# A layer whose first token block is run in two halves of eight feature chunks, with partial sums kept in DRAM

## The chip, the core and the metric

The kernel runs on one core of a Trainium2 chip. The metric is the device time of one execution in microseconds (us). The core has a matrix engine (TensorE, PE in the rows; its weight loads are PEld), two elementwise engines (VectorE is DVE, ScalarE is ACT), GpSimd (POOL), and SyncE (SP), which here only issues DMAs. Each engine works through its own instructions in order. [...]

## What is computed

```python
# attention, per batch b and head h, state is D x D
state = gamma[h] * state + k[t]^T v[t];   y[t] = q[t] @ state / sqrt(D)
x  = y as (B*S = 3072 tokens, H*D = 512)
# layer 1
h  = x @ w_in;   g = h * sigmoid(1.702 * h);          x = g @ w_out
# layer 2 (own weights, a and b are small vectors)
h  = x @ w_in2;  g = P(h) / (Q(h) + 1e-6);            out = g @ w_out2
```

Both layers go from 512 to 2048 features and back. The weights arrive as float64 and are used as float32.

## The kernel before

**Tiling.** The 3072 tokens are cut into 24 chunks of 128 for the attention and into 6 blocks of 512 (four chunks) for the layers. The 2048 features are cut into 16 feature chunks of 128 (`KF` = 16). A *step* is one layer, one block and one feature chunk: 2 x 6 x 16 = 192 steps, numbered j = 0 to 191, layer 1 first. In this text hp*j* and z*j* are the tiles of step j.

**A step.** `g1(j)` multiplies the block's input (a high part `xh` and a low part `xl`) with the chunk's input weights into a PSUM tile `hp`: 12 matmuls of 512 columns. In layer 1, `act1_a` and `act1_b` then make the activation: ACT takes the sigmoid (L367), DVE multiplies it to `z` (L368), ACT rounds `z` to `gh` (L373), and DVE makes the rest `gl` (L374). `g2(i)` multiplies `gh` and `gl` with the output weights, 12 more matmuls, and adds them into four PSUM accumulators `o0` to `o3`. Those have one buffer each. `g1` is issued two steps ahead of `g2` (`lead`). After the last feature chunk of a block, `evac` copies the four accumulators to `os` tiles (two buffers) and stores them to `x2d` in DRAM, from where layer 2 reads them (`load_x2`).

**Weights of layer 1.** 32 units, two for each feature chunk (`wi` and `wo`). Each is loaded as float64 words, turned to float32 by one ACT instruction (L125) and four DVE instructions (L131, L132, L133, L135), and split into two parts by one ACT instruction (L146) and one DVE instruction (L147). `prep(upto)` issues these at two units a step, so that they last for the whole first block.

**Attention of a later block** stands beside the steps of the block ahead of it: `todo` gives each block's four chunks twelve units, kinds T (transposes of q and k), S (scores `pS`, masked by DVE to `sm`, L221) and Y (output `pY`, new state `pK`; DVE makes `xl`, L247, and the state `st`, L252 or L254). Y also loads the chunk two places on and scales its q and k (L186), on POOL for chunks 4 to 7 and on DVE from chunk 8 on. Before, they are spread over the first 13 steps of the block ahead.

**Weights of layer 2** are turned to float32 beside later steps of layer 1, one unit every two steps from step `conv0` = 18 on, and stored to DRAM; during the last block of layer 1 they are loaded again and split.

**Order.** The code gives the order in which the work is traced. SP's DMAs keep that order. The other engines' instructions are put in order by a scheduler when the program is built.

Of the kernel before, what the change touches and what calls it, by code (L numbers as in the profile page):

```python
# [9 lines left out]
F32 = mybir.dt.float32  # L10
# [4 lines left out]
ALU = mybir.AluOpType  # L15
PSUM = bass.MemoryType.PSUM
DRAM = bass.MemoryType.DRAM

P = 128
B, H, S, D = 4, 8, 768, 64  # L20
NT, DM, DFF = B * S, H * D, 2048
# [3 lines left out]
KF = DFF // P  # L25
# [2 lines left out]


def constants():  # L30
    """Identity, causal mask and decay tables: they depend on the shapes alone."""
    gamma = 1.0 - 2.0 ** (-5.0 - np.arange(H, dtype=np.float64))
    t = np.arange(S, dtype=np.float64).reshape(NCH, P)
    up = gamma[None, None, :] ** (t[:, :, None] + 1.0) / np.sqrt(D)
    down = gamma[None, None, :] ** -(t[:, :, None] + 1.0)
    i = np.arange(P)
    c = np.concatenate(
        [
            np.eye(P),
            (i[None, :] >= i[:, None]).astype(np.float64),  # L40
            up.transpose(1, 0, 2).reshape(P, NCH * H),
            down.transpose(1, 0, 2).reshape(P, NCH * H),
        ],
        axis=1,
    )
    return np.ascontiguousarray(c.astype(np.float32))
# [3 lines left out]
def tile_kernel(ctx: ExitStack, tc: tile.TileContext, q, k, v, w1i, w1o, w2i, w2o, pa, pb, cst, out):  # L50
    nc = tc.nc
# [8 lines left out]
    io = ctx.enter_context(tc.tile_pool(name="io", bufs=2))  # L60
# [13 lines left out]
    warm = ws.tile([P, 512], mybir.dt.bfloat16, tag="s", name="warm")  # L74
    st = const.tile([P, NP, P], F32, name="st")

# [1 line left out]
    # A unit is half of what a step needs: 512 columns of the input or of the output weights.  # L78
    dr_w = {}
    for nm, shape in (("i", [DM, DFF]), ("o", [DFF, DM])):  # L80
        dr_w[nm] = dr.tile(shape, F32, name="w2" + nm)
# [10 lines left out]
        return ("i", "o")[u % 2], u // 2  # L92

    def stage_tag(u):
        """The first layer's words wait where the weights of later steps will lie."""
        if u < 16:
            at_slot = 31 - u
        elif u < 24:
            at_slot = 47 - u
        elif u < 28:  # L100
            at_slot = 55 - u
        else:
            return None
        return f"w{at_slot}"
# [56 lines left out]
        nc.sync.dma_start(out=m.rearrange("p (c f) -> p c f", c=KD) if nm == "i" else m, in_=view(nm, dr_w[nm], fc))  # L161
        STG[u] = m

# [1 line left out]
    RAW = {}  # L165
    QK = {}
    SM = {}
# [85 lines left out]
                else:  # L253
                    nc.vector.tensor_copy(out=st[r, :, r], in_=pk[r, :, 0:D])  # L254

# [1 line left out]
    blocks = {1: [4] * 6, 2: [4] * 6}  # L257
    steps = []
    starts = {}
    for layer in (1, 2):  # L260
        t0 = 0
        for bi, n in enumerate(blocks[layer]):
            starts[layer, bi] = t0
            for fc in range(KF):
                steps.append((layer, bi, fc, t0, n * P))
            t0 += n * P
    NS = len(steps)
    first = {(s[0], s[1]): i for i, s in reversed(list(enumerate(steps)))}
    lead = {1: 2, 2: 3}

    x2d = dr.tile([DM, NT], F32, name="x2d")
    HP = {}
    G = {}
    CH = {}
# [24 lines left out]
    def g2(j):  # L299
        layer, bi, fc, t0, n = steps[j]  # L300
        gh, gl = G.pop(j)
        wh, wl = W[layer, "o", fc]
        if fc == 0:
            if layer == 1:
                ACC[layer, bi] = [ps_o.tile([P, n], F32, tag=f"o{d}", name=f"o{j}_{d}") for d in range(KD)]
            else:
                ACC[layer, bi] = [ps_o.tile([P, DM], F32, tag=f"o{d}", name=f"o{j}_{d}") for d in range(n // P)]
        acc = ACC[layer, bi]
        a, z = fc == 0, fc == KF - 1
        for d, o in enumerate(acc):  # L310
            r = slice(d * P, (d + 1) * P)
            if layer == 1:
                nc.tensor.matmul(o, wl[:, r], gh, start=a, stop=False)  # L313
                nc.tensor.matmul(o, wh[:, r], gl, start=False, stop=False)  # L314
                nc.tensor.matmul(o, wh[:, r], gh, start=False, stop=z)  # L315
            else:
                nc.tensor.matmul(o, gl[:, r], wh, start=a, stop=False)  # L317
                nc.tensor.matmul(o, gh[:, r], wl, start=False, stop=False)  # L318
                nc.tensor.matmul(o, gh[:, r], wh, start=False, stop=z)  # L319

    def evac(layer, bi, t0, n):
        acc = ACC.pop((layer, bi))
        if layer == 1:
            for d, o in enumerate(acc):
                t = io.tile([P, 512], F32, tag="o", name=f"os{layer}_{bi}_{d}")
                if d % 2:
                    nc.scalar.copy(out=t[:, :n], in_=o)
                else:
                    nc.vector.tensor_copy(out=t[:, :n], in_=o)  # L329
                nc.sync.dma_start(out=x2d[d * P : (d + 1) * P, t0 : t0 + n], in_=t[:, :n])  # L330
            return
        last = bi == len(blocks[2]) - 1
        for d in range(0, n // P, 2):
            t = ws.tile([P, 2, DM], F32, tag="s", name=f"os{layer}_{bi}_{d}")
            for x in range(2):
                if last and x:
                    nc.vector.tensor_copy(out=t[:, x, :], in_=acc[d + x])
                else:
                    nc.scalar.copy(out=t[:, x, :], in_=acc[d + x])
                if last:  # L340
                    nc.sync.dma_start(out=out[t0 + (d + x) * P : t0 + (d + x + 1) * P, :], in_=t[:, x, :])
            if not last:
                rows = out[t0 + d * P : t0 + (d + 2) * P, :].rearrange("(x p) m -> p x m", p=P)
                nc.sync.dma_start(out=rows, in_=t)
# [61 lines left out]
        gh, gl = G[j]  # L406
        nc.vector.scalar_tensor_tensor(out=gl, in0=p, scalar=-1.0, in1=gh.bitcast(F32), op0=ALU.mult, op1=ALU.subtract)

# [1 line left out]
    todo = [[[], []] for _ in range(NS)]  # L410

    def slot_fn(kind, c, tg, bi, o):
# [14 lines left out]
    chunk = blocks[1][0]  # L427
    for bi in range(1, len(blocks[1])):
        n = blocks[1][bi]
        i0 = first[1, bi - 1]  # L430
        room = KF - lead[1] - 1
        units = [(kind, chunk + x, x * P) for x in range(n) for kind in "TSY"]
        for u, (kind, c, o) in enumerate(units):
            pos = u * 2 * room // len(units)
# [2 lines left out]

    NU = 2 * KF
    prepped = [0]
    # A unit's words are loaded when the unit that lay in their place is done.  # L440
    after_split = {}
    tenant = {}
    early = []
    for u in range(NU):
        t = stage_tag(u)
# [7 lines left out]
            tenant[t] = u  # L453

    def prep(upto):
        """Units of the first layer's weights: three stages, each one unit behind the one before."""
        while prepped[0] < min(upto, NU + 2):
            s = prepped[0]
            if s < NU:
# [9 lines left out]
    with tc.manual_schedule(engines={mybir.EngineType.SP}):  # L469
# [69 lines left out]
        nc.scalar.activation(out=ab[:, 6:7], in_=ab[:, 5:6], func=ACTF.Abs)  # L539
        nxt = 0  # L540
        lastb = first[1, len(blocks[1]) - 1]
        conv0 = KF + 2
        for i in range(-lead[1], NS):
            p0 = 2 * (i + lead[1]) + 5
            prep(p0)
            while nxt < NS and nxt - lead[steps[nxt][0]] <= i:
                j = nxt
# [20 lines left out]
                f()  # L568
            g2(i)
            layer, bi, fc, t0, n = steps[i]  # L570
            if fc == KF - 1:
                evac(layer, bi, t0, n)
            for f in todo[i][1]:
                f()
            # layer 2 weights: to f32 in DRAM
            if i >= conv0 - 4 and i % 2 == 0:
                u = (i - conv0) // 2
                if 0 <= u < NU:
# [2 lines left out]
                    w_store(u)  # L581
                if u + 2 < NU:
                    w_load(2, u + 2)
            # layer 2 weights take the places that the last block of layer 1 leaves
            if lastb <= i:
                f = i - lastb
                for u in (2 * f - 2, 2 * f - 1):
                    if 0 <= u < NU:
                        w_split(2, u)
                    if u + 2 < NU:  # L590
                        w_reload(u + 2)
            # inputs of layer 2
            if lastb <= i:
                nb, off = divmod(i - lastb, KF)
                if nb < len(blocks[2]) and off in (3, 6, 9, 12):
# [28 lines left out]
```

## Time and profile before

| what | value |
|---|---|
| median of 3 runs | 1185.49 us (1184.31 to 1185.55) |
| profiled execution, first to last instruction (its span) | 1183.0 us |
| PE busy | 1168.6 us, 99% of the span |
| DVE busy | 845.7 us, 71% |
| ACT busy | 610.4 us, 52% |
| POOL busy | 15.6 us, 1% |

The runs' times stand 1.3 to 2.6 us above the span of the profiled execution, for which only the span is given. In the profile, "busy" of PE counts a matmul until its modelled end, and matmuls overlap; PEld, the weight loads, do not overlap each other. Idle time of an engine is put down to what released it. A DVE instruction of 0.68 us is followed by the next one 0.60 us later when nothing is waited for, since the two overlap.

### The profile page before, as it was taken

Reading aid. Unit: us, or ns where it says so; the run is one execution under the profiler, and the core shown is the slowest. Engines: PE = TensorE matmul, PEld = TensorE weight load, DVE = VectorE, ACT = ScalarE, POOL = GpSimd, SP = SyncE. Lnnn points to the kernel's source line nnn. Section 1 sums busy time; section 2 is a strip of 40 time slices with the busy share of each in tenths; the row PEclk is TensorE's granted clock in tenths of the full one; section 3 lists DMA queues with packets and bytes.
Section 4 is the critical chain, followed back from the end, with each engine's and each line's share of the span. In section 5 each row is a group of like instructions: output and inputs, shape, how many; then the busy total and the mean of one; then the engine's idle time right before and its main releaser. Section 6 shows DMA issues by size and latency. Waiting matters only on the chain.

```text
span 1183.0 us, 15510 instructions
## 1 busy us (share of the span) xinstructions
PE 1168.6 (99%) x6067; PEld 962.7 (81%) x6067; DVE 845.7 (71%) x1372; ACT 610.4 (52%) x1030; POOL 15.6 (1%) x17
## 2 busy tenths in 40 slices
PE   8899999999999999999999999999999999999998
PEld 5787888888888888888888888888888888888887
DVE  6999945545464554553455898888988988988886
ACT  3555523232233323332344876866766766866765
POOL 1100000000000000000000000000000000000000
PEclk9999999999999999999999999999999999999999
DMA  9944233343342423440343200200200200200000
GB/s 255 308 123 114 63 110 88 89 128 86 81 125 77 126 83 101 122 134 1 115 122 109 73 18 1 72 1 1 72 1 1 71 1 1 71 1 1 36 1 36
DMA packets 128600, 89.26 MB, mean 75 GB/s; under 512 B 78224, under 2 KB 111120, under 8 KB 128528
## 3 DMA queue, kind: packets, MB, share of 16 engines
q1 hardware_dynamic: 128528, 88.28, 25.9%
q8 instruction: 47, 0.77, 0.3%
q14 instruction: 25, 0.20, 0.1%
HBM read 67.29 MB, written 20.97 MB: 75 GB/s over the span
## 4 chain that ended last, share of the span: by engine, by line
PE 90%; DVE 8%; issue 1%; DMA 0%; ACT 0%; SPq 0%; POOL 0%
PE hp L294 14%; PE hp L296 14%; PE hp L295 14%; PE o L317 7%; PE o L319 7%; PE o L318 7%; PE o L313 7%; PE o L315 6%; PE o L314 6%; PE pS L217 2%; PE pY L234 2%; DVE u L133 2%; DVE s L135 1%; PE pY L231 1%; DVE s L131 1%; DVE u L132 1%
## 5 line engine op out<-in xcount | busy, mean ns | idle before, releaser
L294 PE MATMUL hp<-xh,wi 128*128 128x512 f32 x768 | 303.4, 395 | 4.9 <-DVE xl L247 2.7
L296 PE MATMUL hp<-xh,wi 128*128 128x512 f32 x768 | 299.7, 390 | 0.0
L295 PE MATMUL hp<-xl,wi 128*128 128x512 f32 x768 | 299.7, 390 | 0.0
L294 PEld LDWEIGHTS hp<-xh,wi 128*128 128x128 f32 x768 | 144.6, 188 | 38.1 <-DVE wi L147 4.5
L296 PEld LDWEIGHTS hp<-xh,wi 128*128 128x128 f32 x768 | 144.6, 188 | 30.7
L295 PEld LDWEIGHTS hp<-xl,wi 128*128 128x128 f32 x768 | 144.6, 188 | 29.0
L367 ACT ACTIVATE z<-hp 128x512 f32<-128x512 f32 x96 | 57.3, 597 | 211.1 <-PE hp L296 210.8
L368 DVE TENSOR_TENSOR z<-hp,z 128x512 f32<-128x512 f32 x96 | 66.1, 688 | 121.8 <-ACT z L367 121.6
L313 PE MATMUL o<-gh,wo 128*128 128x512 f32 x384 | 152.4, 397 | 0.0
L315 PE MATMUL o<-gh,wo 128*128 128x512 f32 x384 | 150.0, 391 | 0.0
L314 PE MATMUL o<-gl,wo 128*128 128x512 f32 x384 | 149.9, 390 | 0.0
L317 PE MATMUL o<-wo,gl 128*128 128x512 f32 x384 | 149.5, 389 | 0.0
L318 PE MATMUL o<-wo,gh 128*128 128x512 f32 x384 | 149.4, 389 | 0.0
L319 PE MATMUL o<-wo,gh 128*128 128x512 f32 x384 | 149.4, 389 | 0.0
L383 ACT ACTIVATE z<-hp 128x512 f32<-128x512 f32 x96 | 57.4, 598 | 145.2 <-PE hp L296 145.2
L386 DVE SCALAR_TENSOR_TENSOR z<-z,ab,w 128x512 f32<-128x512 f32 x96 | 72.0, 750 | 64.0 <-ACT w L384 63.8
L373 ACT CAST gh<-z 128x512 fp32r<-128x512 f32 x96 | 59.8, 623 | 58.8 <-DVE z L368 58.7
L374 DVE TENSOR_TENSOR gl<-z,gh 128x512 fp32r<-128x512 f32 x96 | 66.1, 688 | 29.3 <-ACT gh L373 28.0
L313 PEld LDWEIGHTS o<-gh,wo 128*128 128x128 f32 x384 | 72.1, 188 | 15.9 <-issue 0.2
L315 PEld LDWEIGHTS o<-gh,wo 128*128 128x128 f32 x384 | 72.1, 188 | 15.3
L317 PEld LDWEIGHTS o<-wo,gl 128*128 128x128 f32 x384 | 72.0, 188 | 15.3 <-DVE os L329 0.4
L318 PEld LDWEIGHTS o<-wo,gh 128*128 128x128 f32 x384 | 72.1, 188 | 15.0
(69 smaller groups left out, 1601.7 us busy)
## 6 DMA issues: line engine op xcount, KB each, us to landing
s<-in_moe_w_in_dram SPq DMA_DIRECT2D x32, 512.0 KB, 6.1
s<-in_moe_w_out_dram SPq DMA_DIRECT2D x32, 512.0 KB, 5.9
rawq<-in_q_dram SPq DMA_DIRECT2D x24, 256.0 KB, 4.7
rawk<-in_k_dram SPq DMA_DIRECT2D x24, 256.0 KB, 3.4
rawv<-in_v_dram SPq DMA_DIRECT2D x24, 256.0 KB, 4.0
x2d<-os SPq DMA_DIRECT2D x24, 256.0 KB, 2.1
x<-x2d SPq DMA_DIRECT2D x24, 256.0 KB, 3.0
out_dram<-os SPq DMA_DIRECT2D x10, 512.0 KB, 3.0
```

Of the source, the lines that this page charges most:

```text
L294: nc.tensor.matmul(hp, wl[:, kk, :], xh[:, kk, :], start=(kk == 0), stop=False)
L295: nc.tensor.matmul(hp, wh[:, kk, :], xl[:, kk, :], start=False, stop=False)
L296: nc.tensor.matmul(hp, wh[:, kk, :], xh[:, kk, :], start=False, stop=(kk == KD - 1))
L313: nc.tensor.matmul(o, wl[:, r], gh, start=a, stop=False)
L314: nc.tensor.matmul(o, wh[:, r], gl, start=False, stop=False)
L315: nc.tensor.matmul(o, wh[:, r], gh, start=False, stop=z)
L317: nc.tensor.matmul(o, gl[:, r], wh, start=a, stop=False)
L318: nc.tensor.matmul(o, gh[:, r], wl, start=False, stop=False)
L319: nc.tensor.matmul(o, gh[:, r], wh, start=False, stop=z)
L368: nc.vector.tensor_tensor(out=z, in0=hp, in1=z, op=ALU.mult)
L374: nc.vector.tensor_tensor(out=gl, in0=z, in1=gh.bitcast(F32), op=ALU.subtract)
L386: nc.vector.scalar_tensor_tensor(out=z, in0=z, scalar=ab[:, 6:7], in1=w, op0=ALU.mult, op1=ALU.add)
```

## The change

Steps are no longer issued block by block from the start. Layer 1 begins with block 0 on feature chunks 0 to 7 (steps 0 to 7), then block 1 on all 16 (steps 8 to 23), then block 0 on feature chunks 8 to 15 (steps 24 to 31). From step 32 on all is as before. After step 7 the four accumulators go to a DRAM tensor `part` by four ACT copies and four stores; after step 31 they are read back, added by DVE to the second half's accumulators, and stored to `x2d`. `prep` issues two units a step up to step 8 and four thirds of a unit a step after that. The attention of block 1 stands beside steps 0 to 4, that of block 2 beside steps 24 to 28 (twelve units in 5 steps, before in 13); blocks 3 to 5 are as before. The conversion of layer 2's weights starts ten steps later.

```diff
+    HALF = KF // 2
+    runs = [(1, 0, 0, HALF), (1, 1, 0, KF), (1, 0, HALF, KF)]
+    runs += [(1, bi, 0, KF) for bi in range(2, 6)] + [(2, bi, 0, KF) for bi in range(6)]
...
+    again = HALF + KF
+    part = dr.tile([DM, 4 * P], F32, name="part")
...
-        a, z = fc == 0, fc == KF - 1
+        a, z = j in opens, j in closes
...
+                if not closes[i]:
+                    nc.scalar.copy(out=t[:, :n], in_=o)
+                    nc.sync.dma_start(out=part[d * P : (d + 1) * P, :], in_=t[:, :n])
+                    continue
+                if bi == 0:
+                    r = io.tile([P, 512], F32, tag="u", name=f"part{d}")
+                    nc.sync.dma_start(out=r, in_=part[d * P : (d + 1) * P, :])
+                    nc.vector.tensor_tensor(out=t[:, :n], in0=o, in1=r, op=ALU.add)
...
-        i0 = first[1, bi - 1]
-        room = KF - lead[1] - 1
+        i0 = again if bi == 2 else first[1, bi - 1]
+        room = (HALF if bi <= 2 else KF) - lead[1] - 1
...
-        conv0 = KF + 2
+        conv0 = again + 4
+        def preps(i):
+            k = i + lead[1]
+            return 2 * k + 5 if k <= HALF else 2 * HALF + 5 + (4 * (k - HALF)) // 3
...
-            p0 = 2 * (i + lead[1]) + 5
+            p0 = preps(i)
```

In the orders below a name's first number is the step, the chunk or the unit; for an accumulator `o` it is the step that opened it and then the quarter; the last number of a name counts tiles.

**DVE at the end of the eighth step.** Before, the rows around z7, the product of step 7:

```order
L221 TENSOR_TENSOR sm1_5_880<-pS1_5_869,cs_93 128x512
L131 TENSOR_SCALAR s1_17_427<-s1_17_427 128x512
L132 TENSOR_SCALAR u17_855<-u17_855 128x512
L147 TENSOR_TENSOR wi1_8_900<-s1_16_416,wi1_8_900 128x512
L133 SCALAR_TENSOR_TENSOR u17_855<-u17_855,s1_17_427 128x512
L368 TENSOR_TENSOR z7_918<-hp7_905,z7_918 128x512
L135 SCALAR_TENSOR_TENSOR s1_17_427<-s1_17_427,u17_855 128x512
```

Now, the rows between z7 and z8, up to the input `xl1_1` that step 8 waits for:

```order
L147 TENSOR_TENSOR wi1_9_1098<-s1_18_465,wi1_9_1098 128x512
L221 TENSOR_TENSOR sm0_7_988<-pS0_7_978,cs_93 128x512
L221 TENSOR_TENSOR sm1_7_990<-pS1_7_979,cs_93 128x512
L186 TENSOR_TENSOR rawq9_1030<-rawq9_1030,cs_93 128x512
L133 SCALAR_TENSOR_TENSOR u19_1065<-u19_1065,s1_19_497 128x512
L131 TENSOR_SCALAR s1_20_512<-s1_20_512 128x512
L135 SCALAR_TENSOR_TENSOR s1_19_497<-s1_19_497,u19_1065 128x512
L132 TENSOR_SCALAR u20_1092<-u20_1092 128x512
L247 TENSOR_TENSOR xl1_1_632<-pY7_1004,xh1_1_631 128x4x128
```

Chunk 7's scores and input, which before stood around steps 13 and 14, now stand ahead of z8, among the same weight units.

**SP at the end of a block.** Before, the four stores of block 1's result stand in a row:

```order
L155 DMA w2i_97<-u6_2328 128x4x128
L116 DMA s2_8_2335<-in_moe2_w_in_dram 128x4x256
L330 DMA x2d_99<-os1_1_0_2369 128x512
L330 DMA x2d_99<-os1_1_1_2372 128x512
L330 DMA x2d_99<-os1_1_2_2375 128x512
L330 DMA x2d_99<-os1_1_3_2378 128x512
L155 DMA w2o_98<-u7_2431 128x512
```

Now, at the end of block 0's second half, the same place in the program (after step 31):

```order
L155 DMA w2o_98<-u1_2300 128x512
L118 DMA s2_3_2307<-in_moe2_w_out_dram 128x1024
L339 DMA part0_2342<-part_100 128x512
L345 DMA x2d_99<-os1_0_15_0_2341 128x512
L339 DMA part1_2347<-part_100 128x512
L345 DMA x2d_99<-os1_0_15_1_2346 128x512
L339 DMA part2_2352<-part_100 128x512
L345 DMA x2d_99<-os1_0_15_2_2351 128x512
L339 DMA part3_2357<-part_100 128x512
L345 DMA x2d_99<-os1_0_15_3_2356 128x512
```

Each of the reads 1 to 3 stands behind a store that waits for the addition ahead of it.

**PE after the same place**, in the out-products of step 32, which need the accumulators that step 31 filled. Before, all four quarters stand together, ahead of the in-product hp35:

```order
L313 MATMUL o32_2_2417<-gh32_2312,wo1_0_424 128x512
L314 MATMUL o32_2_2417<-gl32_2313,wo1_0_424 128x512
L315 MATMUL o32_2_2417<-gh32_2312,wo1_0_424 128x512
L313 MATMUL o32_3_2418<-gh32_2312,wo1_0_424 128x512
L314 MATMUL o32_3_2418<-gl32_2313,wo1_0_424 128x512
L315 MATMUL o32_3_2418<-gh32_2312,wo1_0_424 128x512
L294 MATMUL hp35_2440<-xh1_2_1667,wi1_3_550 128x512
```

Now the third quarter stands behind hp35, and the last one behind chunk 12's scores and three quarters of step 33:

```order
L302 MATMUL hp35_2420<-xh1_2_1884,wi1_3_551 128x512
L319 MATMUL o32_2_2397<-gh32_2284,wo1_0_425 128x512
L320 MATMUL o32_2_2397<-gl32_2285,wo1_0_425 128x512
L321 MATMUL o32_2_2397<-gh32_2284,wo1_0_425 128x512
L217 MATMUL pS0_12_2440<-qT_12_2386,kT_12_2393 128x128
...
L321 MATMUL o32_2_2397<-gh33_2325,wo1_1_494 128x512
L319 MATMUL o32_3_2398<-gh32_2284,wo1_0_425 128x512
L320 MATMUL o32_3_2398<-gl32_2285,wo1_0_425 128x512
L321 MATMUL o32_3_2398<-gh32_2284,wo1_0_425 128x512
```

Two of the four quarters moved back behind other matmuls of PE.

## Rows read from the trace of the kernel before

**Rows 1.** The page, busy time and the span in 40 slices.

```profile
PE 1168.6 (99%) x6067; PEld 962.7 (81%) x6067; DVE 845.7 (71%) x1372; ACT 610.4 (52%) x1030; POOL 15.6 (1%) x17
PE   8899999999999999999999999999999999999998
DVE  6999945545464554553455898888988988988886
PEclk9999999999999999999999999999999999999999
```

**Rows 2.** Busy time by stretch: PE, PEld, DVE, ACT, POOL, clock, DMA.

```profile
40.00:140.00 100.00, 97.86 (x582) 79.14 (x582) 99.68 (x188) 56.99 (x95) 5.24 (x5) 1.00 0.54 160
160.00:260.00 100.00, 100.00 (x596) 82.94 (x595) 52.06 (x89) 29.23 (x49) 0.00 (x0) 1.00 0.34 92
260.00:360.00 100.00, 100.00 (x610) 82.91 (x609) 53.07 (x91) 30.23 (x51) 0.00 (x0) 1.00 0.36 102
360.00:460.00 100.00, 100.00 (x596) 82.74 (x595) 52.07 (x90) 30.58 (x52) 0.00 (x0) 1.00 0.38 106
```

**Rows 3.** Timeline of ACT: sigmoids of steps 0, 16, 32, 79 and 95.

```profile
41.23 0.60 ACT L367 ACTIVATE z<-hp 128x512 f32<-128x512 f32 x1 [1.84 <-PE hp L296]
145.63 0.60 ACT L367 ACTIVATE z<-hp 128x512 f32<-128x512 f32 x1 [0.80 <-PE hp L296]
250.65 0.60 ACT L367 ACTIVATE z<-hp 128x512 f32<-128x512 f32 x1 [2.00 <-PE hp L296]
561.64 0.60 ACT L367 ACTIVATE z<-hp 128x512 f32<-128x512 f32 x1 [3.46 <-PE hp L296]
648.83 0.59 ACT L367 ACTIVATE z<-hp 128x512 f32<-128x512 f32 x1
```

**Rows 4.** Timeline of DVE: products of steps 0, 4 and 7, rows between.

```profile
41.96 0.69 DVE L368 TENSOR_TENSOR z<-hp,z 128x512 f32<-128x512 f32 x1
...
63.24 0.42 DVE L131 TENSOR_SCALAR s<-s 128x512 int32<-128x512 uint32 x1
63.57 0.42 DVE L132 TENSOR_SCALAR u<-u 128x512 f32<-128x512 f32 x1
63.91 0.68 DVE L147 TENSOR_TENSOR wi<-s,wi 128x512 fp32r<-128x512 f32 x1
64.51 0.68 DVE L133 SCALAR_TENSOR_TENSOR u<-u,s 128x512 int32<-128x512 int32 x1
65.11 0.68 DVE L368 TENSOR_TENSOR z<-hp,z 128x512 f32<-128x512 f32 x1
...
86.75 0.68 DVE L368 TENSOR_TENSOR z<-hp,z 128x512 f32<-128x512 f32 x1
```

**Rows 5.** Who waited for in-products: idle time by releaser, line 294.

```profile
  DVE wi L147: 6.6, 10
```

**Rows 6.** Timeline of DVE and POOL: two DVE rows beside a scaling on POOL.

```profile
96.11 1.53 DVE L133 SCALAR_TENSOR_TENSOR u<-u,s 128x512 int32<-128x512 int32 x1
97.56 1.53 DVE L147 TENSOR_TENSOR wo<-s,wo 128x512 fp32r<-128x512 f32 x1
95.60 1.49 POOL L186 TENSOR_TENSOR rawq<-rawq,cs 128x512 f32<-128x512 f32 x1 [24.22 <-DMA rawq<-in_q_dram]
```

**Rows 7.** Timeline of DVE: first and third accumulator copied after step 31.

```profile
257.33 0.68 DVE L329 COPY os<-o 128x512 f32<-128x512 f32 x1
260.20 0.69 DVE L329 COPY os<-o 128x512 f32<-128x512 f32 x1 [1.41 <-DMA x2d<-os]
```

**Rows 8.** DMAs on the page: count, size, median us from issue to landing.

```profile
rawq<-in_q_dram SPq DMA_DIRECT2D x24, 256.0 KB, 4.7
x2d<-os SPq DMA_DIRECT2D x24, 256.0 KB, 2.1
x<-x2d SPq DMA_DIRECT2D x24, 256.0 KB, 3.0
```

**Rows 9.** DMAs of the tensor x2d, writes and reads together, to landing.

```profile
DMA to landing us min/median/max: 2.0/2.6/4.6
```

More of the change, by code (lines that the diff above doesn't have):

```diff
@@ L257, in tile_kernel @@
     blocks = {1: [4] * 6, 2: [4] * 6}
+    HALF = KF // 2
+    starts = {(layer, bi): bi * 4 * P for layer in (1, 2) for bi in range(6)}
+    runs = [(1, 0, 0, HALF), (1, 1, 0, KF), (1, 0, HALF, KF)]
+    runs += [(1, bi, 0, KF) for bi in range(2, 6)] + [(2, bi, 0, KF) for bi in range(6)]
     steps = []
[L259 to L266, printed above, removed]
+    opens, closes = {}, {}
+    for layer, bi, f0, f1 in runs:
+        opens[len(steps)] = True
+        for fc in range(f0, f1):
+            steps.append((layer, bi, fc, starts[layer, bi], blocks[layer][bi] * P))
+        closes[len(steps) - 1] = f1 == KF
     NS = len(steps)
     first = {(s[0], s[1]): i for i, s in reversed(list(enumerate(steps)))}
+    again = HALF + KF
     lead = {1: 2, 2: 3}
     x2d = dr.tile([DM, NT], F32, name="x2d")
+    part = dr.tile([DM, 4 * P], F32, name="part")
     HP = {}
@@ L302, in g2 @@
         wh, wl = W[layer, "o", fc]
-        if fc == 0:
+        if j in opens:
             if layer == 1:
@@ L319, in g2, with evac @@
                 nc.tensor.matmul(o, gh[:, r], wh, start=False, stop=z)
-    def evac(layer, bi, t0, n):
+    def evac(i):
+        layer, bi, fc, t0, n = steps[i]
         acc = ACC.pop((layer, bi))
@@ L324, in evac @@
             for d, o in enumerate(acc):
-                t = io.tile([P, 512], F32, tag="o", name=f"os{layer}_{bi}_{d}")
-                if d % 2:
+                t = io.tile([P, 512], F32, tag="o", name=f"os{layer}_{bi}_{fc}_{d}")
+                if not closes[i]:
[6 more added lines that the diff above has]
+                    nc.vector.tensor_tensor(out=t[:, :n], in0=o, in1=r, op=ALU.add)
+                elif d % 2:
                     nc.scalar.copy(out=t[:, :n], in_=o)
@@ L570, in tile_kernel @@
             layer, bi, fc, t0, n = steps[i]
-            if fc == KF - 1:
-                evac(layer, bi, t0, n)
+            if i in closes:
+                evac(i)
             for f in todo[i][1]:
```

## The prediction

> **What bounds the kernel now.** I read the page first. PE is busy for 99% of the span at full clock, DVE for 71%; but in slices 2 to 5 DVE stands at 9 where it later stands at 4 to 6 [rows 1]. That is block 0 of layer 1 with its 32 weight units. Then the stretches: from 40 to 140 us DVE is busy for 99.68 of 100 us, in the three stretches behind it for 52 to 53 [rows 2]. So the question is what PE loses while DVE is full. For this I take the sigmoids on ACT, which follow the in-products. The last block, without attention beside it, takes 648.83 - 561.64 = 87.2 us for 16 steps: 5.45 a step, 2.72 for twelve matmuls. A block with four chunks of attention takes 250.65 - 145.63 = 105.0, so a chunk costs PE 17.8 / 4 = 4.45 us. Block 0 takes 145.63 - 41.23 = 104.4 [rows 3]; but by the order only 14 out-products stand in that stretch and not 16, so it should take 105.0 - 2 x 2.72 = 99.6. Block 0 loses 4.8 us. The weight loads say nearly the same: 79.14 us against 82.9 in the full stretches, a shortfall of 3.7, which is 4.5 us at that rate [rows 2]. In-products wait for `wi` from DVE ten times [rows 5]. So 4.8 us, 0.4% of the kernel, is all that easing DVE in block 0 can give; everywhere else PE is full.
>
> Busy PE alone would say less: it is idle for 2.1 of those 100 us. [...]
>
> **First half and block 1.** A weight unit is two short DVE instructions, followed by the next after 0.335 us, and three long ones, after 0.60 [rows 4]. Up to step 8 the change still issues two units a step, and it puts block 1's attention, before spread over 13 steps, into the first five. So DVE's list up to `wi` of step 7, counted in the order from z0 on, is 52 long ones, 21 short ones and a pair of state updates (0.9): 31.2 + 7.0 + 0.9 = 39.1 us. The same count for the kernel before, up to z7 (58, 25, one pair), gives 44.1; the trace has 86.75 - 41.96 = 44.8 [rows 4], so the method holds. To it come 1.7 us where POOL scales a chunk and two DVE rows take 1.53 instead of 0.68 [rows 6], and about 0.7 (my estimate from 0.6 us rows) in which DVE waits for chunk 4's output, which is now wanted earlier: hp7 can begin at 41.5 us behind z0. PE's own work up to there is six in-products, 5.33 out-products and two chunks: 16.3 + 14.5 + 8.9 = 39.7, less 0.7 for its start ahead of z0: 39.0. PE still waits 2.5 us. From hp7 on PE leads: up to the end of hp16 it has ten in-products, 8.67 out-products and two chunks, 27.2 + 23.6 + 8.9 = 59.7 us, while DVE's list from z7 to z8 is 15.5 us and less than 5 us a step behind that. In this stretch PE waits three times in a row for DVE (chunk 6's `sm`, step 7's `gl`, chunk 7's `xl`), which stands behind weight units: some 0.5 each, 1.6 in all. The end is 41.5 + 59.7 + 1.6 = 102.8 behind z0, 103.5 behind the end of hp0, against 104.4. **Gain 1 us.** Bounds: 4.8, when nothing of the loss is left; or a loss of 2, when each of the three hand-overs costs a long row's 0.6 us twice more. I take the counted value.
>
> Block 1 then has no attention, and DVE has at most 4/3 of a unit and two products a step, 3.3 + 1.2 = 4.5 of 5.45 us: PE is full. The first half's four copies and stores lie behind hp8, hp9 and hp10 (8 us of matmuls); a copy is 0.68 [rows 7] and a store lands in 2.1 [rows 8], two rounds of it in 5.6. Cost 0; without that cover, 3.
>
> **The second half's end.** Before, the third accumulator is copied 2.87 us after the first [rows 7]; no matmul waits for it. Now four reads of 256 KB, four additions and four stores. SP keeps the code's order, so reads 1 to 3 can only go out when the addition ahead has been made. The nearest row is `x<-x2d`, the same size: 3.0 us [rows 8]. Count from the start of step 31's out-products. z33 comes first on DVE, addition 0 ends at 2.1; the store and read 1 go out by 2.6, it lands at 5.6, addition 1 ends at 6.3; read 2 lands at 9.9, addition 2 ends at 10.7; read 3 lands at 14.2, addition 3 ends at 14.9. PE has out-products and hp34 (5.4), two transposes (0.7), and then wants quarter 0 at 6.1, quarter 1 at 6.8, with hp35 behind it quarter 2 at 10.2, and with the scores and nine matmuls quarter 3 at 14.4, with the wait of 0.5 in it. So it waits 0.5 + 0.5, with semaphores 1.2 us. **Cost 1.2.** Bounds by the fastest and slowest transfer on x2d, 2.0 and 4.6 [rows 9]: 0, and 1.1 + 2.5 + 1.3 = 4.9 us. Behind the waiting addition stand, on DVE, chunk 12's second mask and a weight unit; a step's product has three runs of twelve matmuls, 8.2 us, less 1.3 for sigmoid and product, until PE wants its buffer, so nobody waits for those.
>
> [...]
>
> **The dense attention beside steps 24 to 28.** PE has 8 x 5.45 + 17.8 = 61.4 us of work there and DVE far less. What can wait is a chain: on DVE, chunk 13's scaling stands ahead of chunk 11's masking and waits for a load of 4.7 us [rows 8] that goes out once chunk 11 is transposed. PE has hp30, the scores, twelve matmuls and the output's first part meanwhile, 2.7 + 1.1 + 2.7 + 1.0 = 7.5 us; the masking ends at about 7.7. Four chunks: 0.5 us; bounds 0 and 3 (a landing 1.5 us later at two of them).
>
> **Layer 2's weights ten steps later** now overlap with the reloads in the last block, and both use the same three buffers. Reloads come later, but the first is wanted 12 steps on; the closest is the last quarter of layer 2's first input, whose split now stands behind z95 and is wanted by the last three matmuls of hp96. Cost 0.2, bounds 0 and 2.
>
> **Sum.** -1.0 + 0 + 1.2 + 0.5 + 0.2 = +0.9 us on a span of 1183.0. The runs lie 1.3 to 2.6 above that span, so I add it to their median: 1185.5 + 0.9 = **1186.4 us**. A measurement of this kernel can tell 0.2% (2.4 us) from no change; this is within it.
>
> **Rivals.** *Faster:* the DVE list is more even than I count, the scheduler's order hides the hand-overs, and all of the 4.8 us comes back, with 0.8 for the rest: 1181.5. For it: DVE is the one thing PE waits for in block 0 [rows 5]. Against it: in the first seven steps the list per step has not become shorter but longer, 39.1 us up to hp7 against 39.0 of PE's work.
> *Slower, by the reads:* each read goes out behind a store and beside loads of weights and chunks, and lands as the slowest on x2d, 4.6 us. Then the end of block 0 costs 4.9 instead of 1.2: 1190.1. It decides from about 3.8 us a read, where it costs 2.5 more. For it: three reads in a chain on one in-order queue. Against it: the median of 3.0.
> *Slower, by the dense attention:* in both places (steps 0 to 4, 24 to 28) each of eight chunks costs PE 0.6 us more at a hand-over: +4.8, 1191. Against it: the order leaves twelve matmuls between most of the hand-overs.
>
> **Chances.** Forecast 0.56, faster 0.14, reads 0.18, dense attention 0.12. The forecast's own range is 1183.5 to 1188.5; its few cases beyond 0.2% about make up for those of the rivals that stay within it. So faster 0.14, same 0.56, slower 0.30. To leave out no more than 2 in 10, the range goes to 1182.5 below (about half of the faster case is outside) and 1190.5 above.
>
> **What would show it.** In the profile after: the sigmoids of steps 0 and 16 some 103.5 us apart (99 to 100 if the faster case holds); weight loads still short in the first 50 us behind z0 and full from about step 10 on; DVE at 9 up to about 65 us behind z0 and then at 8; reads of `part` that land in about 3 us, and matmuls of line 319 that wait for DVE's line 340 by about 1 us in all. It would be wrong if PE waits by more than 3 us around steps 31 to 33 or between steps 24 and 30, or if block 0 loses nothing any more.

## The result and the profile after

The changed kernel takes 1192.86 us (median of 4 runs, 1191.57 to 1193.98); the kernel before, beside it, 1185.24. The ratio is 1.0066, interval 1.0051 to 1.0080: slower by 7.6 us, where 0.9 was forecast and the range ended at 1190.5. The profiled execution has a span of 1191.8 us, against 1183.0. These two executions stand 8.8 us apart and not 7.6, since single executions vary: the four of the changed kernel took 1191.57 to 1193.98 us, and the profiled one is the longest of them.

From the page of after, in answer to [rows 1]:

```profile
PE 1173.7 (98%) x6067; PEld 964.8 (81%) x6067; DVE 847.8 (71%) x1374; ACT 608.6 (51%) x1032; POOL 15.6 (1%) x17
DVE  5999923547464554562356898888888988988886
PEclk9999999999999999999999899999999999999999
```

DVE's full stretch is slices 2 to 5 as before, with a gap now behind it (slices 6 and 7), where block 1 runs without attention. What is new for PE is one digit: the granted clock of slice 23 (655 to 685 us) is 8. To find the place, the sigmoids of steps 0, 16, 24, 32 and 80, as in [rows 3]:

```profile
40.98 0.60 ACT L382 ACTIVATE z<-hp 128x512 f32<-128x512 f32 x1
...
146.44 0.59 ACT L382 ACTIVATE z<-hp 128x512 f32<-128x512 f32 x1
...
189.93 0.60 ACT L382 ACTIVATE z<-hp 128x512 f32<-128x512 f32 x1 [3.46 <-PE hp L302]
...
252.33 0.60 ACT L382 ACTIVATE z<-hp 128x512 f32<-128x512 f32 x1 [3.52 <-PE hp L302]
...
569.35 0.60 ACT L382 ACTIVATE z<-hp 128x512 f32<-128x512 f32 x1 [3.46 <-PE hp L302]
```

The kernel before has the sigmoid of step 80 here:

```profile
567.08 0.60 ACT L367 ACTIVATE z<-hp 128x512 f32<-128x512 f32 x1 [3.46 <-PE hp L296]
```

From step 0 to step 80 it is 528.37 us against 525.85 before: 2.5 us lost by the split and all that lies near it (1.1 of them up to step 16, 1.5 behind it). From step 80 to the end of the span it is 1191.8 - 569.35 = 622.45 against 1183.0 - 567.08 = 615.92: **6.5 us are lost behind step 80**, where the split itself has long been over. All of them lie in two stretches of 10 us (columns as in [rows 2]). Before had PE busy for 10.00 us at a clock of 1.00 in both, as in this row of it:

```profile
650.00:660.00 10.00, 10.00 (x46) 8.28 (x45) 7.36 (x12) 8.71 (x14) 0.00 (x0) 1.00 0.06 22
```

The changed kernel:

```profile
650.00:660.00 10.00, 6.59 (x21) 4.68 (x20) 7.09 (x12) 6.73 (x13) 0.00 (x0) 0.77 0.72 206
660.00:670.00 10.00, 10.00 (x41) 8.15 (x40) 7.21 (x12) 8.05 (x13) 0.00 (x0) 0.89 0.02 7
```

PE's own rows there (start, duration, and in brackets the idle time and its releaser) show what happens:

```profile
652.50 0.39 PE L302 MATMUL hp<-xh,wi 128*128 128x512 f32 x1
656.17 0.80 PE L300 MATMUL hp<-xh,wi 128*128 128x512 f32 x1 [3.28 <-ACT xh L368]
657.10 0.80 PE L301 MATMUL hp<-xl,wi 128*128 128x512 f32 x1
657.69 0.63 PE L302 MATMUL hp<-xh,wi 128*128 128x512 f32 x1
658.12 0.63 PE L319 MATMUL o<-gh,wo 128*128 128x512 f32 x1
...
662.75 0.39 PE L300 MATMUL hp<-xh,wi 128*128 128x512 f32 x1
```

The first in-product of layer 2 has nine of its twelve matmuls done and waits 3.28 us for the last quarter of its input. Then 15 matmuls take 662.75 - 656.17 = 6.58 us, which at the usual 0.227 us would be 3.4 (nine of them ahead of the wait start within 1.81 us, from 650.69 to 652.50). Most of the 15 start 0.43 us apart, nearly twice that; the granted clock of that stretch is 0.50:

```profile
656.00:662.00 6.00, 5.70 (x13) 4.14 (x14) 4.71 (x8) 4.82 (x8) 0.00 (x0) 0.50 0.46 131
```

The wait is 3.28 us from the modelled end of the ninth matmul, and 0.17 more from where the next one would have started, since matmuls overlap. With the 3.18 us lost behind it this is 3.28 + 0.17 + 3.18 = 6.6 us: the whole loss.

Why the quarter is late is told by SP's queue (L161 reloads a weight unit of layer 2, L367 loads a quarter):

```profile
594.47 0.37 SPq L161 DMA_DIRECT2D r<-w2i  x1
599.17 0.32 SPq L161 DMA_DIRECT2D r<-w2o  x1
603.30 0.37 SPq L161 DMA_DIRECT2D r<-w2i  x1
607.41 0.32 SPq L161 DMA_DIRECT2D r<-w2o  x1
607.78 0.43 SPq L367 DMA_DIRECT2D x<-x2d  x1
...
651.85 0.42 SPq L367 DMA_DIRECT2D x<-x2d  x1
```

A step needs two reloads in 5.45 us; here one goes out every 4.1 to 4.7 us, each waiting until the one ahead has landed and been split (from 565 to 657 us SP's waits at line 161 name a reload's landing with 20.4 us and its split, line 147, with 21.3). The other two of the three buffers of that pool are held by float64 words whose conversion is not yet done (DVE has touched them at 586.34 and 596.16, ACT turns them to float32 at 606.56 and 612.13). SP issues in order, so all behind a reload is late with it: the last quarter goes out at 651.85, 82.5 us behind the sigmoid of step 80; before at 637.03, 69.95 behind it:

```profile
637.03 0.42 SPq L352 DMA_DIRECT2D x<-x2d  x1
```

The lateness is not the same all the way. Against step 80, the four quarters go out 15.6, 21.8, 19.3 and 12.5 us later than before: as the last words are converted (628.94 and 640.47) and their buffers come free, the reloads catch up, and from 631.63 to 651.48 they go out every 1.8 us on average.

### The profile page after: what moved, and what is told of

The parts are those of the page before. It is cut to its first block, busy times and chain, and to the rows that moved or that the text cites. A ratio compares the mean times of both kernels' runs of the same rounds, so it can differ in the third digit from the quotient of the medians.

```text
span 1191.8 us, 15527 instructions
## 1 busy us (share of the span) xinstructions
PE 1173.7 (98%) x6067; PEld 964.8 (81%) x6067; DVE 847.8 (71%) x1374; ACT 608.6 (51%) x1032; POOL 15.6 (1%) x17
## 4 chain that ended last, share of the span: by engine, by line
PE 88%; DVE 7%; DMA 3%; ACT 1%; issue 1%; SPq 0%; ACTq 0%; DVEq 0%
PE hp L300 13%; PE hp L301 13%; PE hp L302 13%; PE o L323 7%; PE o L325 7%; PE o L324 7%; PE o L319 6%; PE o L321 6%; PE o L320 6%; DMA r<-w2o 2%; PE pY L234 2%; PE pS L217 2%; PE pY L231 1%; DVE s L135 1%; DVE u L133 1%; DVE wo L147 1%
## 5 line engine op out<-in xcount | busy, mean ns | idle before, releaser
L319 PEld LDWEIGHTS o<-gh,wo 128*128 128x128 f32 x384 | 72.7, 189 | 17.1 <-DVE os L340 0.7
L321 PEld LDWEIGHTS o<-gh,wo 128*128 128x128 f32 x384 | 72.5, 189 | 15.6 <-issue 0.2
L320 PEld LDWEIGHTS o<-gl,wo 128*128 128x128 f32 x384 | 72.7, 189 | 14.6 <-DVE gl L389 0.2
```

## The experiments

My theory after this reading: the conversion ten steps later costs some 6.5 us, by buffers shared with the reloads; the split itself costs 1 to 2.5. Rival: the split costs the time, and the gap at step 96 only shows it. The table has all kernels that were timed in several runs (7, 8 and 11 ran once, for their profiles); the last three columns come from their profiles: from the sigmoid of step 0 to that of step 80, from there to the span's end, and from there to the issue of the last x2 quarter.

| kernel | median us | ratio to before | 0 to 80 | 80 to end | quarter |
|---|---|---|---|---|---|
| before | 1184.6 to 1185.2 | | 525.85 | 615.9 | 69.95 |
| after | 1192.86 | 1.0066 [1.0051, 1.0080] | 528.37 | 622.5 | 82.5 |
| 1 conversion at 18 | 1186.45 | 1.0011 [1.0002, 1.0020] | 526.91 | 617.3 | 72.4 |
| 2 before, conversion at 28 | 1190.33 | 1.0049 [1.0036, 1.0061] | 527.06 | 624.2 | 84.1 |
| 3 quarters asked for earlier | 1189.57 | 1.0042 [1.0030, 1.0055] | 527.31 | 621.2 | 81.3 |
| 4 reloads in other buffers | 1185.92 | 1.0009 [1.0000, 1.0018] | 526.87 | 615.6 | 58.8 |
| 5 gap filled | 1191.79 | 1.0060 [1.0047, 1.0074] | 528.39 | 621.4 | 82.5 |
| 6 conversion at 24 | 1186.09 | 1.0015 [1.0006, 1.0024] | 527.26 | 616.0 | 72.7 |
| 9 before, other unit order | 1184.40 | 0.9997 [0.9989, 1.0006] | 527.15 | 615.6 | |
| 10 as 4, other unit order | 1185.98 | 1.0010 [1.0001, 1.0019] | 528.59 | 616.1 | |
| 12 as 4, reads by two | 1184.93 | 1.0002 [0.9993, 1.0011] | 527.12 | 615.6 | |

How much the first stretch varies by itself is told by kernel 2, which has before's code up to step 14: between the sigmoids of steps 0 and 16 it takes 105.60 us, and before 104.40. From step 16 to step 80 the two agree (421.46 and 421.45), and behind step 80 undisturbed kernels have 615.6 to 616.1.

**1. The late conversion undone, the split kept.**

```diff
-        conv0 = again + 4
+        conv0 = KF + 2
```

> The changed kernel with the conversion of layer 2's weights back at step 18 instead of 28; the two parts of block 0 stay. Theory (the late conversion costs the last block of layer 1 about 6.5 us: 3.4 us of waiting in hp96 and some 3.2 us of matmuls at half clock behind it, and the split itself about 2.3 us): median 1186.5 to 1188, and no wait of PE for the split of the last x2 quarter. Rival (the split, that is the partial sums' reads and the dense attention, costs the time, and the gap at hp96 only takes up a delay that would show elsewhere): 1191 to 1193.

Measured 1186.45, 1.8 us above before: 5 to 6 us of the 7.6 are gone with this one line, and no wait for the quarter is left. The rival falls. In this profile 1.0 us of the 1.4 that remain behind step 80 is a wait of layer 2's first out-products for the accumulators (DVE, line 344), which the kernels 4 and 6 do not show.

**2. The late conversion alone, in the kernel before.**

```diff
-        conv0 = KF + 2
+        conv0 = KF + 12
```

> The kernel before, block 0 in one piece, with the conversion of layer 2's weights at step 28 instead of 18: that part of the change alone. Theory: the same gap at hp96, 6 to 7 us slower than before, 1191 to 1192.5. Rival (the split costs the time): within 1.5 us of before, 1184 to 1187.

Measured 1190.33, 5.7 us slower, somewhat under the expected 1191. The list of PE's waits has the same entry as after, a little longer:

```profile
PE hp L294 <- ACT xh L353: 4.3, 1, 4.3
```

So the loss needs no split at all. The two parts add up: 5.7 alone, and 1.8 for the split without it, make 7.5. In the profiled execution of this kernel the loss behind step 80 is larger, 624.2 - 615.9 = 8.3 us; its sigmoid of step 0 came 3.4 us earlier than the one before, and so its span is only 6.1 longer. One profiled execution is no measure of the whole time; the 5.7 of the medians is.

**3. The quarters asked for earlier in the code** (steps 81, 83, 85, 87).

```diff
-                if nb < len(blocks[2]) and off in (3, 6, 9, 12):
-                    load_x2(nb, (off - 3) // 3)
+                at_off = (1, 3, 5, 7) if nb == 0 else (3, 6, 9, 12)
+                if nb < len(blocks[2]) and off in at_off:
+                    load_x2(nb, at_off.index(off))
```

> The changed kernel, conversion still at step 28, with the four loads of layer 2's first input at steps 81, 83, 85 and 87 instead of 83, 86, 89 and 92. Theory: the serial reloads stay, but the last quarter is split long before hp96 wants it, so the 3.3 us wait and the half clock behind it both go: 1186 to 1188. Rival A (the reloads themselves come too late for PE, the quarter only came last): PE waits for the weights of step 96 instead, 1190 to 1193. Rival B (the clock falls there without the wait): only 3.3 us come back, 1189 to 1190.

Measured 1189.57: the theory as I put it missed. Five steps earlier in the code made the last quarter's issue only 1.2 us earlier (81.3 instead of 82.5 us behind step 80), because it still stands in SP's queue behind the reloads of its step, and these are late. PE still waits for it, and 25 us later once more, for DVE's polynomial (line 417), which is late by then too:

```profile
653.64 0.50 PE L300 MATMUL hp<-xh,wi 128*128 128x512 f32 x1 [1.38 <-ACT xh L368]
...
678.15 0.50 PE L300 MATMUL hp<-xh,wi 128*128 128x512 f32 x1 [1.78 <-DVE p L417]
...
679.92 0.63 PE L324 MATMUL o<-wo,gh 128*128 128x512 f32 x1
```

The time is near that of rival B, but not by its mechanism: the matmuls did not slow behind the first wait (0.23 to 0.24 us apart from 653.97 on), they slowed behind the second (0.42 to 0.43 apart from 679.92 to 682.91).

**4. The reloads in buffers of their own** (the six of the chunks' words, which are empty by then), conversion still at step 28.

```diff
-        s = ws.tile([P, DM, 2], I32, tag="s", name=f"r{u}")
-        m = s.rearrange("p f t -> p (f t)")[:, 0:DM].bitcast(F32)
+        m = at.tile([P, DM], F32, tag="raw", name=f"r{u}")
```

> The changed kernel, conversion still at step 28, with the reloads of layer 2's weights in the six buffers of the chunks' words, which are empty in the last block, instead of the three that the conversion's loads also hold. Theory (the shared buffers make the reloads serial, and that delays the quarter): reloads two a step again, ACT waits for none of them, 1186 to 1188. Rival (the words of the last conversions and the reloads compete for the DMA itself or for ACT and DVE): the quarter is still late and 1190 to 1193.

Measured 1185.92, with 615.6 us behind step 80 as undisturbed. SP's queue at the start of the last block (L160 is the reload here, L366 the quarter):

```profile
580.52 0.58 SPq L160 DMA_DIRECT2D r<-w2i  x1
581.20 0.61 SPq L160 DMA_DIRECT2D r<-w2o  x1
581.86 0.63 SPq L160 DMA_DIRECT2D r<-w2i  x1
582.58 0.46 SPq L160 DMA_DIRECT2D r<-w2o  x1
...
626.99 0.42 SPq L366 DMA_DIRECT2D x<-x2d  x1
```

Four reloads go out within 2.1 us, and the last quarter 23.7 us earlier, behind step 80, than in the changed kernel. The same words and the same conversions run beside them, so neither the DMA nor ACT nor DVE was what made the reloads slow: it was the buffers.

**5. The gap filled with matmuls that nobody reads.**

```diff
...
+            if fill is not None and kk == KD - 1:
+                for _ in range(14):
+                    nc.tensor.matmul(fill, wh[:, 0, :], xh[:, 0, :], start=True, stop=True)
```

> The changed kernel with 14 matmuls more, whose product is read by nobody, put into the place where PE waited 3.3 us in hp96 (14 x 0.227 = 3.2 us), and nothing else changed; the last x2 quarter is as late as in the changed kernel. Theory (the matmuls behind the wait ran at half clock because PE had stood still): the clock stays at 1.00 from 650 to 670 us, the matmuls behind the gap stand 0.227 us apart, and some 3.2 us come back: 1189 to 1190.5. Rival (the clock falls there for another reason, such as the load of the other engines or of the DMA at that place): half clock as before, and no gain, 1192 to 1193.5.

PE's rows, and the stretches to 670 us:

```profile
649.93 3.33 PE L305 MATMUL fill<-xh,wi 128*128 128x512 f32 x14
653.64 0.49 PE L306 MATMUL hp<-xh,wi 128*128 128x512 f32 x1 [0.38 <-ACT xh L374]
654.57 0.50 PE L307 MATMUL hp<-xl,wi 128*128 128x512 f32 x1 [0.43 <-DVE xl L375]
...
657.69 0.39 PE L327 MATMUL o<-gh,wo 128*128 128x512 f32 x1
657.91 0.39 PE L306 MATMUL hp<-xh,wi 128*128 128x512 f32 x1
```

```profile
650.00:660.00 10.00, 9.19 (x40) 7.03 (x39) 7.37 (x11) 7.40 (x13) 0.00 (x0) 1.00 0.51 156
660.00:670.00 10.00, 10.00 (x46) 8.29 (x45) 8.90 (x15) 8.67 (x15) 0.00 (x0) 1.00 0.00 1
```

The quarter is as late as in the changed kernel (82.5), the clock stays at 1.00, and the matmuls behind the gap are about 0.23 us apart again, against 0.43 in the changed kernel. DVE and ACT are as busy from 650 to 660 us as in the changed kernel (7.37 and 7.40 us against 7.09 and 6.73). So the half rate came from PE's standing still and not from the load of the others at that place. But the time did not come back as expected: 1191.79, and 621.4 us behind step 80 instead of 622.5, some 1.1 us where 3.2 were expected. The 15 matmuls behind the gap take 2.3 us less (4.27 us from 653.64 to the next in-product at 657.91). The other 0.9 of the 3.18 was for the most part not the clock: the second matmul also waits for the quarter's low part from DVE, and starts 0.93 us behind the first in both kernels. Further, the first matmul behind the gap starts 0.3 us later, and PE waits again from some 18 us on (9.43 of 10 us busy from 670 to 680, where the changed kernel has 10.00), for the accumulators that DVE copies (line 350), as in run 1: with PE sooner, the next late thing is met.

**6. The conversion four steps earlier than in the change.**

```diff
-        conv0 = again + 4
+        conv0 = again
```

> The changed kernel with the conversion from step 24 instead of 28: its last word loads are issued at step 82 and its last unit is converted at step 86, so it shares the three buffers with the reloads for 6 steps instead of 10. Theory (each step of overlap makes the reloads later, and only what is left of the lateness at hp96 costs): the last quarter is split before hp96 wants it, PE does not wait, 1186 to 1188. Rival (any overlap costs, in proportion): 6 tenths of 6.5 us stay, 1189.5 to 1191.

Measured 1186.09, and PE does not wait behind step 80. Six steps of sharing make the quarter 2.7 us later than in before and cost nothing; ten make it 12.5 us later and cost 6.5. It is a threshold: PE has done its nine matmuls 83.4 us behind step 80 (652.73 - 569.35), and from the quarter's issue to its first matmul 3.6 (run 3) to 4.6 us (runs 2 and 5) pass; so by this estimate an issue by about 79 is in time. The kernels with 58.8 to 72.7 pay nothing, those with 81.3, 82.5 and 84.1 wait 1.4, 3.3 and 4.3 us.

**7, 8, 11 and 12: the price of the split itself,** from the version of run 4, by the sigmoids of steps 24 and 40, which stand 115.29 us apart there:

```profile
188.76 0.60 ACT L381 ACTIVATE z<-hp 128x512 f32<-128x512 f32 x1 [3.46 <-PE hp L301]
...
304.05 0.60 ACT L381 ACTIVATE z<-hp 128x512 f32<-128x512 f32 x1 [5.61 <-PE hp L301]
```

Run 7 leaves the reads out:

```diff
-                    r = io.tile([P, 512], F32, tag="u", name=f"part{d}")
-                    nc.sync.dma_start(out=r, in_=part[d * P : (d + 1) * P, :])
-                    nc.vector.tensor_tensor(out=t[:, :n], in0=o, in1=r, op=ALU.add)
+                    nc.vector.tensor_copy(out=t[:, :n], in_=o)
```

> The version with the reloads in buffers of their own, without the four reads of the partial sums: the accumulators of the second half are only copied, as in the kernel before, so that block 0's output lacks the first eight feature chunks. Prediction on record (the reads cost PE 1.2 us between steps 32 and 36): the sigmoids of steps 32 and 36 stand 23.4 us apart instead of 24.58. Rival (the reads are hidden, and the copies themselves or the attention cost what is lost there): 24.3 to 24.6 as with them.

```profile
188.64 0.60 ACT L379 ACTIVATE z<-hp 128x512 f32<-128x512 f32 x1 [3.46 <-PE hp L301]
...
303.33 0.60 ACT L379 ACTIVATE z<-hp 128x512 f32<-128x512 f32 x1 [5.61 <-PE hp L301]
```

114.69: the reads cost 0.6 us, half of the 1.2 forecast. (The pair 32 and 36 that I had named is of no use: without the reads ACT reaches the sigmoid of step 32 later.) Run 11 keeps two reads under way:

```diff
+                    for e in range(2) if d == 0 else [d + 1] if d in (1, 2) else []:
+                        r = io.tile([P, 512], F32, tag="u", name=f"part{e}")
+                        nc.sync.dma_start(out=r, in_=part[e * P : (e + 1) * P, :])
+                        PT.append(r)
+                    r = PT[d]
```

> The version with the reloads in buffers of their own, with two reads of the partial sums under way at a time instead of one: reads 0 and 1 are issued together, read 2 and 3 ahead of the additions 1 and 2. Theory (the reads cost 0.6 us between steps 24 and 40, by the run without them, because each is issued only after the addition ahead): the sigmoids of steps 24 and 40 come 114.7 to 114.9 us apart instead of 115.29. Rival (the first read's 3 us, or DVE's four additions, cost it): 115.2 to 115.3.

```profile
188.72 0.60 ACT L385 ACTIVATE z<-hp 128x512 f32<-128x512 f32 x1 [3.46 <-PE hp L302]
...
303.42 0.60 ACT L385 ACTIVATE z<-hp 128x512 f32<-128x512 f32 x1 [5.61 <-PE hp L302]
```

114.70: the 0.6 us are all back, as the theory expected. It is the order of issue that cost them. Run 8 gives the attention beside each half of block 0 six steps instead of five:

```diff
-        room = (HALF if bi <= 2 else KF) - lead[1] - 1
+        room = HALF - lead[1] if bi <= 2 else KF - lead[1] - 1
```

> The version with the reloads in buffers of their own, with the four chunks of attention that stand beside each half of block 0 spread over six steps instead of five. Theory (dense attention costs about 1 us beside the second half, by hand-overs that are too close): the sigmoids of steps 24 and 32 come 61.4 to 61.9 us apart instead of 62.4; beside the first half DVE is full, so the sigmoids of steps 0 and 16 stay at 103.9 (103.5 to 104.5). Rival (the room does not matter, the chain of a chunk does; and a last chunk one step later makes hp8 and hp32 wait): 62.4 or more, and 0 to 16 up by 1.

Sigmoids 24 and 40 come at 187.54 and 302.84 us, 115.30 apart: no difference (the sigmoid of step 32, which I had named, is displaced here too). Sigmoids 0 and 16 stand 105.06 apart, above the 103.5 to 104.5 expected but within what that stretch varies. One step more of room does not give back the remaining 1.0 us; whether a looser placing would, and which link of a chunk's chain costs it, was not tried. Run 12 times run 11's kernel:

> The version with the reloads in buffers of their own and two reads of the partial sums under way, timed. Theory (what is left of the change's cost is some 1 us of dense attention beside the second half, and nothing in the first half): 0 to 1.5 us above the kernel before, ratio 1.000 to 1.0012. Rival (the first half does ease DVE by the 1 us that the prediction counted): equal or faster, ratio 0.9985 to 1.000.

Measured 1184.93 against 1184.79, ratio 1.0002 [0.9993, 1.0011]. With the buffers and the reads mended, the medians, which can tell about 1 us here, show neither a cost of the split nor a gain. The stretch that repeats best still shows a cost: from the sigmoid of step 16 to that of step 80 runs 11 and 12 take 422.34 us, the kernel before 421.45, so 0.9 us stay lost there.

**9 and 10: another order of the weight units,** to see whether the 4.8 us that block 0 loses can be had by delaying what PE wants late.

```diff
     def unit(u):
-        return ("i", "o")[u % 2], u // 2
+        if u < 2:
+            return "i", u
+        if u >= 30:
+            return "o", u - 16
+        return ("i", u // 2 + 1) if u % 2 == 0 else ("o", u // 2 - 1)
...
-            p0 = 2 * (i + lead[1]) + 5
+            p0 = 2 * (i + lead[1]) + 3
```

> The kernel before, undivided, with layer 1's weight units prepared in another order: the output weights of a step, wanted two steps after its input weights, come two steps later (i0, i1, i2, o0, i3, o1, ... o14, o15), and the list runs two units less ahead. Theory (in block 0 PE loses 4.8 us because DVE's list is full, as the prediction says; two units are some 5 us of DVE): the sigmoids of steps 0 and 16 come 3 to 4.5 us closer, 100 to 101.5 instead of 104.4, and the median falls to 1180.5 to 1182. Rival (DVE's hand-overs, not the length of its list, hold PE up): 103.5 or more, and no change of the median.

> The changed kernel with the reloads in buffers of their own and the same order of the weight units as in the run with the undivided block. Theory: the first half's list is shorter by two units up to step 7, which PE waited for; the sigmoids of steps 0 and 16 come 100 to 101.5 apart instead of 104 to 105.5, median 1181.5 to 1183.5, and the loss behind step 24 (1.6 us) stays, so that it is 0.5 to 2 us slower than the undivided block in that order. Rival: as there, no change, 1185 to 1187.

Both missed; run 10 has 105.7 between sigmoids 0 and 16 and the median of run 4. Sigmoids 0 and 16 of run 9:

```profile
39.83 0.58 ACT L371 ACTIVATE z<-hp 128x512 f32<-128x512 f32 x1
...
144.57 0.60 ACT L371 ACTIVATE z<-hp 128x512 f32<-128x512 f32 x1 [0.48 <-PE hp L300]
```

104.7, as before. The expectation had a fault of its own: a list that is shifted by two units still has two units a step between steps 0 and 16, so only its start could move; it came 1.4 us earlier, within what this start varies between profiles (37.8 to 41.4). I have no version that beats both kernels.

## The prediction, step by step

**What bounds the kernel** held as far as it went: PE is full outside block 0 [rows 2], and DVE is what it waits for there [rows 5]. But from it I concluded where the change could cost something, and looked least where PE was full and every other queue had room.

**First half and block 1, -1.0 us.** Forecast 103.5 between sigmoids 0 and 16. The changed kernel's profile has 105.46 (41.0 to 146.4); the nine profiles with this first half and its order of the units (after and runs 1, 3 to 7, 11, 12) have 103.9 to 105.6, on average 104.7; the two with the undivided one and that order (before, run 2) 104.4 and 105.6. So the gain is at most some 0.3 us, and less than the variation. The count itself nearly held: in-product hp7 was to begin 41.5 us behind z0, and begins 85.23 - 42.67 = 42.6 behind it in the changed kernel's profile. DVE's rows of 1.53 us there are three, and the count had two:

```profile
42.67 0.69 DVE L383 TENSOR_TENSOR z<-hp,z 128x512 f32<-128x512 f32 x1
...
68.66 1.53 DVE L135 SCALAR_TENSOR_TENSOR s<-s,u 128x512 int32<-128x512 int32 x1
...
72.24 1.53 DVE L133 SCALAR_TENSOR_TENSOR u<-u,s 128x512 int32<-128x512 int32 x1
73.69 1.53 DVE L389 TENSOR_TENSOR gl<-z,gh 128x512 fp32r<-128x512 f32 x1
...
85.23 0.50 PE L300 MATMUL hp<-xh,wi 128*128 128x512 f32 x1 [0.70 <-DVE wi L147]
```

From hp7 to sigmoid 16 it is 61.2 us, 61.3 by the count. The other 1.0 us of the difference lies at the start: z0 stands 1.7 us behind sigmoid 0, and 0.7 in the kernel before. One of the readings that were to show the forecast failed: DVE did not fall to 8 some 65 us behind z0, it was busy for 99.31 of the 100 us from 40 to 140.

**Partial stores, 0.** Held: no entry of PE's waits names their copies.

**The second half's end, +1.2 us.** Right in mechanism, but sized at twice what it is: the reads cost 0.6 us (runs 4, 7 and 11). PE's waits name line 340 once, with 0.3 us, where about 1 was forecast, and for the 0.2 of the 1.2 that was put down to semaphores no run has a row. The chain ran much as counted; the four additions, which were to end 4.2 to 4.4 us apart:

```profile
259.01 0.68 DVE L340 TENSOR_TENSOR os<-o,part 128x512 f32<-128x512 f32 x1
...
262.94 0.69 DVE L340 TENSOR_TENSOR os<-o,part 128x512 f32<-128x512 f32 x1 [2.47 <-DMA part<-part]
...
266.91 0.69 DVE L340 TENSOR_TENSOR os<-o,part 128x512 f32<-128x512 f32 x1 [0.88 <-DMA part<-part]
...
271.69 0.68 DVE L340 TENSOR_TENSOR os<-o,part 128x512 f32<-128x512 f32 x1
```

They start 3.9, 4.0 and 4.8 us apart. The two that wait for their reads start 2.8 and 2.9 us behind the reads' issue (260.14 and 264.04); the count had 3.0.

**The dense attention, +0.5 us.** Steps 24 to 32 take 252.33 - 189.93 = 62.4 us in the changed kernel, 61.4 by the count of its work: 1.0, within the bounds of 0 and 3. The 0.9 us that run 12 still loses between steps 16 and 80 agree with it; what in the chain costs it stays open.

**Layer 2's weights ten steps later, +0.2 us, bounds 0 and 2.** This is the step that failed: it measured 6.5 us in the profile and 5.7 alone (run 2). It named the right place, the shared three buffers and the last quarter in hp96, but priced it by where the load stands in the code. I did not follow SP's queue: with two buffers held by words, the reloads pass one after another through the third. The direction could have been had from rows before the change: a transfer of that size lands in 3.0 us [rows 8], an ACT and a DVE instruction then need 0.6 each [rows 3, 4], so 4.2 a reload and 8.4 a step that has 5.45, 3 us of lateness for each step of sharing. The quarter had some 9 us of slack (79 against 69.95, run 6). The count would have gone too far, to 30 us for ten steps, where the quarters were 12.5 to 21.8 late, since two buffers are held by words only in part of that time; but a wait it would have shown. The upper bound failed for the same reason, and for one more: behind the wait of 3.28 us PE ran at half rate (0.43 us apart), some 2.3 us on top of the 3.4 of standing still (run 5).

The sum by what was measured: -0.3 + 0 + 0.6 + 1.0 + 6.5 = 7.8 us; the medians differ by 7.6. **The rivals**, all in the first 36 steps, did not come about. The faster one would have needed block 0's 4.8 us back; 104.7 instead of 99.6 between sigmoids 0 and 16 says that nearly all of it is still lost. The third rival's 1191 lies near the measured time by luck: in both its places together the dense attention cost some 1 us and not 4.8. Nor did any of the conditions come about that were named for being wrong: they all looked at the first 36 steps, and the loss lies at step 96.

## What to carry to other kernels

When a change lets two streams of loads overlap that share rotating buffers, count the buffers that the slower stream holds, and price the other by one transfer and its release after another; then follow the in-order queue that issues both, since everything behind a load that waits for a buffer is late too, wherever the code asks for it (here the last quarter, by 12.5 us). Asking earlier in the code (run 3, 1.2 us earlier out) then helps little, and other buffers (run 4, 23.7 us earlier out) mend it all. And look at edits that seem to be bookkeeping as closely as at the idea of the change: here a start index cost 6 us, and the split itself, when mended, none that the medians show.

## What the runs showed of the hardware

In the changed kernel a wait of PE cost more than itself: 3.28 us of it, and 3.18 behind it, some 2.3 of these by matmuls at half rate (by run 5; the granted clock was 0.50 from 656 to 662 us). Behind 3.3 and 4.3 us of waiting (after, run 2) the next matmul already ran at half rate (0.80 us long, against 0.49 and 0.50 in runs 5 and 3), and about twelve did (ten gaps between their starts are 0.42 or 0.43 us); behind 1.4 us (run 3) and behind 0.4 and 0.4 us with one matmul between them (run 5) none did. In run 3 the first matmuls behind a wait of 1.78 us were 0.23 to 0.34 us apart, and the half rate came 1.8 us later, from 679.92 on (0.42 to 0.43 us apart up to 682.91), where PE was busy again; so here the matmul that shows it was not the one behind the gap.
